# Filters re-read with both planes per transfer, second weights read two rows at a time, first weights taken at column stride two

## The chip, the cores and the metric

The kernel runs on one core of a Trainium2 chip. The core has a matrix engine (TensorE, with its own row for weight loads), VectorE, ScalarE and GpSimd for elementwise work, and SyncE, which issues most of the transfers. The metric is the device time of one execution in microseconds (us); lower is better. In the profile the engines are called PE, PEld (weight loads), DVE, ACT, POOL and SP; a "q" behind an engine's name means its instruction queue rather than its arithmetic, and most transfers have only such a row.

## The reference

Two steps follow one another. The first filters each of 8 sequences of 3008 positions and 256 channels in the frequency domain; the second is a two-layer perceptron with an exact GELU on all 24064 rows.

```python
X = np.fft.rfft(x, axis=1)
F = (filt_r + 1j * filt_i)[None, :, :]
y = np.fft.irfft(X * F, n=x.shape[1], axis=1)     # 8 x 3008 x 256
x = y.reshape(B * S, D)                            # 24064 x 256
h = x @ w_in                                       # 256 x 2048
g = 0.5 * h * (1.0 + erf(h * inv_sqrt2))
return g @ w_out                                   # 2048 x 256
```

## The kernel before

**Filtering.** The transform of length 3008 is split as 47 x 64 and done with matrix products against tables. Sequence 0 goes first, all on its own (functions c1 to c4). Sequences 1 to 7 are worked while TensorE does the perceptron of earlier rows: s1 (product with the 47-point table, L397), a round trip through device memory in the buffer R (written at L407, read back by r1 at L413 into b_sb), s2 (product with the 64-point table T2p, L421, and at L424 the multiplication by the filters F), s3 (L438), a second round trip (written at L450, read back by r2 at L457 into d_sb), and s4 (L466), which writes the filtered rows to a ring buffer, y_sb.

**Filters.** F holds, for each of 24 frequency columns k, two planes t (real and imaginary part) of 256 channels, over 128 partitions. At the start the filters are loaded in one order of partitions, for sequence 0. A copy is saved to device memory (Fd, L106) and later read back in another order by load_filters_again (L113), in groups of 32 partitions. It is called three times during the perceptron of the first rows: for columns 0 to 3, 4 to 7, and 8 to 23.

**Perceptron.** Rows go in 47 tiles of 512. For a tile, mm1 (L580) makes one of 16 blocks of 128 hidden columns per call: two matmuls of 512 columns, one for each half of the 256 input channels, whose weights are 128 columns of w_in_sb; ScalarE applies the GELU into g_sb (L583). The second layer runs one tile behind. For tile 0 it is mm2 (L594), plain. For all others it is mm2_seven (L653): the product is split in 2 x 2 blocks and computed with seven block products instead of eight. The sums over g_sb are made on VectorE (L622, L628, L635), the sums over the weights once, by weight_sums (L608), into w_sums. Each 128-column matmul has its own weight load. The hidden blocks jc = 2i and 2i + 1 form the two halves of the 2 x 2 split.

**Order.** The order is written out by hand. A slot s is one call of mm1; `at[s]` lists what is put ahead of it, then comes the second layer of the tile before (seven 128-column matmuls), then mm1. SP's queue carries the filter reads, b_sb, d_sb, the writes of R and the outputs, in program order. GpSimd's queue carries the loads that convert from float32: x, w_in, w_out. Around slot 12 the order on SP is: 4 writes of R, filters 0 to 3, three b_sb reads, filters 4 to 7, filters 8 to 23.

```python
put(r1 if c < 3 else unit(3) + 1, m.r1, b, c)   # r1 = 12 for b = 1
...
put(11, m.load_filters_again, 0, 4)
put(13, m.load_filters_again, 4, 4)
put(17, m.load_filters_again, 8, 16)
put(17, m.weight_sums)
```

The second weights are loaded by two calls of load_w_out on GpSimd (L138), right after the loads of x for sequence 1. The table T4a is made on GpSimd (L376, L378) in the same stretch, from 49.17 to 73.87 us.

Of the kernel before, what the change touches and what calls it, by code (L numbers as in the profile page):

```python
# [30 lines left out]
class _Mix:  # L31
# [75 lines left out]

    def load_filters_again(self, k0, k):

        for t in range(2):  # L110
            for o in range(0, 128, 32):
                i = self.st["Fd"][o // 64, :, :, t, k0:k0 + k, :].rearrange("q i k c -> (q i) (k c)")
                self.nc.sync.dma_start(out=self.F[o:o + 32, t, k0:k0 + k, :], in_=i)  # L113

    def dup_filters(self, eng, k0, k):
        for k in range(k0, k0 + k, 2):
# [17 lines left out]
            self.nc.gpsimd.dma_start(out=self.w_in_sb[:, dc, :], in_=wi[:, dc, :])  # L134

    def load_w_out(self, j):
        wo = self.w_out.rearrange("(jc p) o -> p jc o", p=128)
        self.nc.gpsimd.dma_start(out=self.w_out_sb[:, j:j + 8, :], in_=wo[:, j:j + 8, :])  # L138


    def iota(self, g, name, shape, pattern, base=0, cm=0, dt=FP32):
# [430 lines left out]
    def mm1(self, t, jc):  # L572
        nc = self.nc
        if jc == 0:
            self.st["g", t] = self.pg.tile([128, 16, TCH], FP16, tag="g", name="g_sb")
        ps = self.bank("ps_h", "h")
        o = 0
        for off, n in self.segs(t):
            for dc in range(2):
                nc.tensor.matmul(ps[:, o:o + n], lhsT=self.w_in_sb[:, dc, jc * 128:jc * 128 + 128],  # L580
                                 rhs=self.ring[:, dc, off:off + n], start=(dc == 0), stop=(dc == 1))
            o += n
        nc.scalar.activation(out=self.st["g", t][:, jc, :], in_=ps, func=AF.Gelu)  # L583
# [330 lines left out]
```

## Time and profile before

| What | Value |
|---|---|
| Median of 4 runs | 753.81 us (752.76 to 754.97) |
| The profiled execution | 752.93 us |
| Its span in the profile | 751.1 us |
| TensorE clock granted | 0.999 of full speed |
| L580, matmuls of the first layer | 417.9 us busy, 1468 recorded |
| L580, weight loads | 1600, 98 ns each |
| L653, matmuls of the second layer | 219 ns each as recorded, groups that overlap |
| Filter reads F<-Fd | 8 of 256 KB (5.8 us to landing), 16 of 64 KB (2.2 us) |
| b_sb<-R | 28 of 384 KB, 4.2 us to landing |
| w_out_sb | 2 of 512 KB, 11.2 us to landing |

The span runs from the first to the last recorded instruction. "Busy" counts the time in which at least one instruction of an engine is running. A matmul's recorded length includes its way through the array, so that matmuls overlap in the record: seven of the second layer, 219 ns each, take 0.55 us together. "To landing" is the median time from a transfer's issue to its arrival. A wait is put down to what came last before the waiting instruction started, by the profile's semaphore events. The whole program of a stage must be read from the timeline of that stage; shares of busy time are averages over all of them.

### The profile page before, as it was taken

To read this page: it belongs to the slowest core of one execution; us is meant where nothing else is said; L and a number is where in the kernel's file an instruction comes from. 1 tells how busy PE (TensorE), PEld (TensorE's weight loads), DVE (VectorE), ACT (ScalarE), POOL (GpSimd) and SP (SyncE) were. 2 spreads that over 40 slices of the span, in tenths; PEclk is the share of its full clock that TensorE was granted. 3 is DMA by queue.
4 is the path that set the end of the run, shared out by engine and by line. 5 is a ranking of instruction groups with operands and counts; after the bars stand their busy time and mean duration, and the time that the engine had idled before them with its cause. 6 is when DMAs were issued, how large, how long until landed. Compare 5 with 4: busy or idle time off the path is not lost.

```text
span 751.1 us, 20124 instructions
## 1 busy us (share of the span) xinstructions
PE 728.3 (97%) x8284; PEld 518.1 (69%) x8420; DVE 593.0 (79%) x1065; ACT 544.6 (73%) x963; POOL 101.9 (14%) x191
## 2 busy tenths in 40 slices
PE   7998999999999999999999999999999999999997
PEld 4845676766776767666677666666677766777776
DVE  7967978897787977789777997779967898675566
ACT  6895678677786777866777667876678767777773
POOL 7969100020001200012000120002100000000000
PEclk9999999999999999999999999999999999999999
DMA  9999663474445652546525457245562433511011
GB/s 146 221 195 271 148 141 93 121 173 103 103 114 154 140 130 84 145 124 127 143 73 161 112 106 169 61 145 123 122 142 76 130 106 86 114 44 42 30 57 58
DMA packets 92605, 90.73 MB, mean 121 GB/s; under 512 B 7904, under 2 KB 79072, under 8 KB 92256
## 3 DMA queue, kind: packets, MB, share of 16 engines
q1 hardware_dynamic: 84128, 73.43, 35.5%
q0 software_dynamic: 8384, 16.00, 14.1%
q8 instruction: 66, 1.08, 0.6%
q14 instruction: 27, 0.22, 0.1%
HBM read 57.15 MB, written 48.23 MB: 140 GB/s over the span
## 4 chain that ended last, share of the span: by engine, by line
PE 86%; DVE 6%; DMA 3%; ACT 2%; issue 2%; SPq 1%; POOL 0%; DVEq 0%; POOLq 0%; ACTq 0%
PE ps_o L653 37%; PE ps_h L580 36%; PE ps_s L466 3%; PE ps_s L438 3%; PE ps_s L421 2%; PE ps_s L397 2%; DVE p L424 2%; DVE s_sb L622 1%; ACT g_sb L583 1%; DMA x_sb<-in_x_dram 1%; DMA F<-Fd 1%; PE ps_c L528 1%; DMA b_sb<-R 1%; DVE ost L682 1%; PE ps_c3t L543 1%
## 5 line engine op out<-in xcount | busy, mean ns | idle before, releaser
L583 ACT ACTIVATE g_sb<-ps_h 128x512 f16<-128x512 f32 x752 | 447.9, 597 | 185.7 <-PE ps_h L580 165.4
L580 PE MATMUL ps_h<-y_sb,w_in_sb 128*128 128x512 bf16 (+3 forms) x1468 | 417.9, 365 | 0.4
L653 PEld LDWEIGHTS <-g_sb 128*128 128x128 f16 x2944 | 193.9, 98 | 80.7 <-issue 15.6
L653 PEld LDWEIGHTS <-s_sb 128*128 128x128 f16 x2208 | 150.2, 98 | 51.3 <-issue 2.9
L580 PEld LDWEIGHTS <-w_in_sb 128*128 128x128 bf16 x1600 | 124.6, 98 | 6.6 <-issue 1.0
L653 PE MATMUL ps_o<-w_sums,g_sb 128*128 128x128 f16 x1472 | 127.1, 219 | 2.0 <-DVE g_sb L628 1.2
L653 PE MATMUL ps_o<-w_sums,s_sb 128*128 128x128 f16 x1472 | 126.5, 219 | 1.3
L622 DVE TENSOR_TENSOR s_sb<-g_sb 128x1024 f16<-128x1024 f16 x184 | 122.9, 691 | 0.0
L653 PE MATMUL ps_o<-w_out_sb,g_sb 128*128 128x128 f16 x1472 | 120.3, 219 | 1.8
L424 DVE TENSOR_TENSOR p<-ps_s,F 128x1024 bf16<-128x1024 f32 x84 | 102.4, 1220 | 24.7 <-PE ps_s L421 14.6
L123 POOL COPY gate<-p 1x1 bf16<-1x1 bf16 x40 | 19.1, 477 | 417.6 <-DVE p L424 417.6
L628 DVE TENSOR_TENSOR g_sb<-s_sb,g_sb 128x1024 f16<-128x1024 f16 x92 | 63.6, 691 | 1.1
L653 PE MATMUL ps_o<-w_out_sb,s_sb 128*128 128x128 f16 x736 | 63.3, 219 | 0.5
L635 DVE TENSOR_TENSOR s_sb<-g_sb 128x1024 f16<-128x1024 f16 x92 | 62.7, 681 | 0.0
L304 DVE TENSOR_SCALAR y_sb<-ps_s 128x376 bf16<-128x376 f32 x56 | 30.5, 545 | 27.9 <-PE ps_s L466 27.9
L675 DVE TENSOR_TENSOR t_sb<-t_sb,ps_o 128x256 f32<-128x256 f32 x46 | 19.2, 417 | 40.0 <-PE ps_o L653 40.0
L466 PEld LDWEIGHTS <-d_sb 96*128 96x128 bf16 x448 | 31.4, 98 | 25.7 <-issue 0.7
L302 DVE CAST a_sb<-ps_s 128x512 bf16<-128x512 f32 x57 | 36.6, 686 | 13.0 <-PE ps_s L397 12.8
L670 DVE TENSOR_TENSOR ost<-t_sb,ps_o 128x256 f32<-128x256 f32 x46 | 19.2, 418 | 31.0 <-PE ps_o L653 31.0
L466 PE MATMUL ps_s<-T4a,d_sb 96*128 96x94 bf16 x448 | 37.2, 206 | 1.8 <-DMA d_sb<-R 0.5
L682 DVE TENSOR_TENSOR ost<-t_sb,ps_o 128x256 f32<-128x256 f32 x90 | 33.6, 414 | 5.6 <-PE ps_o L653 5.6
L421 PE MATMUL ps_s<-b_sb,T2p 128*128 128x256 bf16 x168 | 32.1, 273 | 4.3 <-DMA b_sb<-R 3.2
(147 smaller groups left out, 502.5 us busy)
## 6 DMA issues: line engine op xcount, KB each, us to landing
out_dram<-ost SPq DMA_DIRECT2D x92, 256.0 KB, 2.6
x_sb<-in_x_dram POOLq DMA_DIRECT2D x64, 188.0 KB, 3.8
b_sb<-R SPq DMA_DIRECT2D x28, 384.0 KB, 4.2
R<-v_sb SPq DMA_DIRECT2D x84, 128.0 KB, 2.5
d_sb<-R SPq DMA_DIRECT2D x56, 192.0 KB, 3.9
R<-a_sb SPq DMA_DIRECT2D x108, 96.0 KB, 2.2
F<-Fd SPq DMA_DIRECT2D x8, 256.0 KB, 5.8
Fd<-F SPq DMA_DIRECT2D x8, 192.0 KB, 6.8
```

Source lines behind the costliest of these rows:

```text
L302: self.nc.vector.tensor_copy(out=out, in_=in_)
L304: self.nc.vector.tensor_scalar(out=out, in0=in_, scalar1=scale, scalar2=None, op0=ALU.mult)
L421: nc.tensor.matmul(ps[:, 256 * i:256 * i + 256], lhsT=self.T2p[:, k].rearrange("p a b c d -> p (a b c d)"), rhs=self.st[b, "b", k // 6][:, ...
L424: nc.vector.tensor_tensor(out=w, in0=ps.unsqueeze(1).to_broadcast([128, 2, 512]), in1=self.F[:, :, 2 * p:2 * p + 2, :].rearrange("p t a b ...
L466: nc.tensor.matmul(ps[:, 94 * i:94 * i + 94], lhsT=d[:, (grp % 2) * 4 + i, 128 * half:128 * half + 128], rhs=self.T4a[:, 4 * grp + i], sta ...
L580: nc.tensor.matmul(ps[:, o:o + n], lhsT=self.w_in_sb[:, dc, jc * 128:jc * 128 + 128], rhs=self.ring[:, dc, off:off + n], start=(dc == 0), ...
L583: nc.scalar.activation(out=self.st["g", t][:, jc, :], in_=ps, func=AF.Gelu)
L622: self.nc.vector.tensor_tensor(out=self.st["s", t][:, i:i + 2], in0=a, in1=b, op=ALU.subtract)
L628: self.nc.vector.tensor_tensor(out=a21[:, k], in0=self.st["s", t][:, k, 0], in1=a22[:, k], op=ALU.add)
L635: self.nc.vector.tensor_tensor(out=self.st["s4", t][:, k], in0=a12[:, k], in1=s2[:, k], op=ALU.subtract)
L653: nc.tensor.matmul(ps[:, (m + 1) % 2, sub, :], lhsT=a[:, i, 128 * sub:128 * sub + 128], rhs=b[:, i], start=i == 0, stop=i == 7)
L682: v(out=c(h, 1 - h), in0=tt, in1=p, op=ALU.add)
```

## The change

Three edits. load_filters_again makes one transfer for both planes of 32 partitions instead of one for each plane, so four issues a call instead of eight. load_w_out reads two neighbouring rows of w_out in one run: partition p of block pair i now holds rows 256 i + 2 p and 256 i + 2 p + 1, where before block jc held rows 128 jc + p. So that h has its columns in the same order, mm1 takes every second of 256 weight columns, starting at jc % 2.

```diff
     def load_filters_again(self, k0, k):
-        for t in range(2):
-            for o in range(0, 128, 32):
-                i = self.st["Fd"][o // 64, :, :, t, k0:k0 + k, :].rearrange("q i k c -> (q i) (k c)")
-                self.nc.sync.dma_start(out=self.F[o:o + 32, t, k0:k0 + k, :], in_=i)
+        for o in range(0, 128, 32):
+            i = self.st["Fd"][o // 64, :, :, :, k0:k0 + k, :].rearrange("q i t k c -> (q i) t (k c)")
+            self.nc.sync.dma_start(out=self.F[o:o + 32, :, k0:k0 + k, :], in_=i)
...
     def load_w_out(self, j):
-        wo = self.w_out.rearrange("(jc p) o -> p jc o", p=128)
-        self.nc.gpsimd.dma_start(out=self.w_out_sb[:, j:j + 8, :], in_=wo[:, j:j + 8, :])
+        wo = self.w_out.rearrange("(i p e) o -> p i (e o)", p=128, e=2)
+        self.nc.gpsimd.dma_start(out=self.w_out_sb[:, j:j + 8, :].rearrange("p (i e) o -> p i (e o)", e=2),
+                                 in_=wo[:, j // 2:j // 2 + 4, :])
...
         ps = self.bank("ps_h", "h")
+        w = self.w_in_sb[:, :, 256 * (jc // 2) + jc % 2:256 * (jc // 2) + 256:2]
         o = 0
         for off, n in self.segs(t):
             for dc in range(2):
-                nc.tensor.matmul(ps[:, o:o + n], lhsT=self.w_in_sb[:, dc, jc * 128:jc * 128 + 128],
+                nc.tensor.matmul(ps[:, o:o + n], lhsT=w[:, dc],
                                  rhs=self.ring[:, dc, off:off + n], start=(dc == 0), stop=(dc == 1))
```

## The prediction

> **What bounds the kernel now.** I read the page's first part, then the chain of waits that ended last, then TensorE's waits over the whole run and by stage, and last the timeline of the stage in which the filters come back.
>
> ```profile
> PE 728.3 (97%) x8284; PEld 518.1 (69%) x8420; DVE 593.0 (79%) x1065; ACT 544.6 (73%) x963; POOL 101.9 (14%) x191
> ...
> PE 86%; DVE 6%; DMA 3%; ACT 2%; issue 2%; SPq 1%; POOL 0%; DVEq 0%; POOLq 0%; ACTq 0%
> ```
>
> TensorE is busy 728.3 of 751.1 us, and 86% of the chain is TensorE. So time is lost or won in two ways only: by a wait of TensorE, or by a change in the pace at which it runs. The list of waits has few of the first kind. After 50 us TensorE stands still for long just three times, and the two that matter lie in the stage that the change touches:
>
> ```profile
> PE ps_s L421 <- DMA b_sb<-R: 3.2, 1, 3.2
> PE ps_o L653 <- DVE g_sb L628: 0.8, 1, 0.8
> ```
>
> (Columns: total us, times, longest us; the third is 0.5 us for d_sb, much later.) The first lasts from 55.4 to 58.58 us. What it waits for is seen on SP's own queue, timeline from 44 to 100 us:
>
> ```profile
> 49.34 1.92 SPq L407 DMA_DIRECT2D R<-p  x4
> 51.31 3.71 SPq L113 DMA_DIRECT2D F<-Fd  x8
> 55.12 1.32 SPq L413 DMA_DIRECT2D b_sb<-R  x3
> 56.53 8.36 SPq L113 DMA_DIRECT2D F<-Fd  x16
> ```
>
> SP issues in order. The first eight filter reads take 3.71 us, 0.46 each, and only then comes the b_sb read that TensorE needs. It lands about 3.4 us after its issue (3.3 is the least, 3.6 the median of the first two), at 58.5.
>
> **Part 1, the filters' return.** Each call makes four issues instead of eight: 24 become 12, with the same bytes and the same runs. An issue's cost hardly depends on its bytes (0.42 to 0.46 us apart at 64 KB and at 256 KB), so I price a 128 KB issue at 0.46; a third dimension in the pattern may cost more, and the nearest rows, Fd<-F with its reversed rows, take 0.59 at the median. The first call then takes 4 x 0.46 = 1.84 us, and b_sb can be issued at 51.31 + 1.84 = 53.2 instead of 55.12. Is something else late then? b_sb reads what R<-p wrote. The last of those four is issued at about 50.84 and takes 2.2 us to land: 53.0. So the issue holds at 53.2, 1.9 us earlier. But the 512 KB of the first call now go out in half the time and stand ahead of b_sb in the same queue. Between 64 and 71 us, where nearly only filters move, they run at some 220 GB/s with the engines full. From 51.9 at that rate the 512 KB last until 54.3, so the data of b_sb start about 0.5 us later than on a free queue. Gain at this wait: 1.9 - 0.5 = **1.4 us**. Ends: 0.9 if an issue costs 0.59 (4 x 0.13 = 0.5 less), 1.9 if the backlog does not matter.
>
> The other filters: SP held its sixteenth filter read until 60.87, when the third b_sb landed, and the last call's 2.1 MB landed at 70.7. After the change that call begins some 2 to 3 us earlier and still needs 2.1 MB / 220 GB/s = 9.5 us, so it lands near 68.4. Its first reader is the product of unit 4, which ran on VectorE at 72.96, behind other work of VectorE. Nothing gates there before or after. The chain names 6.25 us of "F<-Fd" ahead of L628, but VectorE had no idle time before L628, and L628 does not read F; I book nothing for it.
>
> What is given back: VectorE runs without a gap from 65.9 to 76 us, and three L622 and one L628 in it take 1.1 to 1.2 us instead of 0.68 while GpSimd makes T4a (49.2 to 73.9). GpSimd's work does not move. With TensorE and VectorE 1.4 us earlier, the next L622 (at 72.32) and L628 (at 74.10), now 0.7 each, come under GpSimd's last operations and may lose 0.45 each. The second L628 is what the 0.8 us wait is for, so 0 to 0.9 goes back into it; I take 0.4. Part 1: -1.4 + 0.4 = **-1.0 us**, between -1.9 and 0.
>
> **Part 2, the second weights in pairs of rows.** Two GpSimd issues (0.90 and 0.92 us) with half the runs. They land 10.0 and 12.4 us after 33.7 and 34.6, the last at 47.0; the first reader, L608, starts at 47.83, just as VectorE is done with the p copies ahead of it. GpSimd then waits 6.4 us for t_sb at 49.17, which hides whatever its issues save or cost. Loads of x are ahead in the queue. Worth 0; without that cover, some tenths of a us. Row order in w_out_sb and column order of h change together, so L608, L653 and the sums keep count and shape.
>
> **Part 3, weight columns at stride two.** No instruction is added. But all 1,600 loads of w_in_sb now step over every second column, and nothing in this trace loads weights with a step. This is the term that decides, because of where the load stands:
>
> ```profile
> 98.31 0.28 PE L653 MATMUL ps_o<-w_out_sb,s_sb 128*128 128x128 f16 x2
> ...
> 98.37 0.15 PEld L580 LDWEIGHTS <-w_in_sb 128*128 128x128 bf16 x2
> 98.42 0.38 PE L580 MATMUL ps_h<-y_sb,w_in_sb 128*128 128x512 bf16 x1
> ```
>
> (Timeline; columns: start us, us, what. Groups of x2 start some 0.055 us apart.) A load starts when the matmul before it starts. The second load of a slot has a 512-column matmul over it (0.215 us from start to start): twice its 98 ns would still be hidden. The first has only the last 128-column matmul of L653, 0.055 us. There are 720 such slots (tiles 2 to 46, sixteen each), so every 10 ns not hidden cost 7.2 us. Bounds by rows of the same engine:
>
> ```profile
> L580 PEld LDWEIGHTS <-w_in_sb 128*128 128x128 bf16 x1600 | 124.6, 98 | 6.6 <-issue 1.0 <-DMA x_sb<-in_x_dram 0.4
> ...
> L438 PEld LDWEIGHTS <-U 64*64 64x64 bf16 x336 | 7.9, 106 | 13.1 <-issue 8.9
> ...
> L356 PEld LDWEIGHTS <-T2g 128*96 128x96 bf16 x1 | 0.1, 119 | 0.0
> ```
>
> (After the bar: busy us, mean ns of one.) The 128-column load is faster than the 96-column one: full-width loads go a quicker way. Without it, 64 and 96 columns give 13 ns per 32, so 128 would take 132, 34 more than now. Exposed in full that is 720 x 34 = 24.5 us; exposed not at all, 0. A gain has a reason against it: same number of weights, and the array's 55 ns per matmul is the pace.
>
> [...]
>
> **Sum and rivals.** Against the profiled execution (752.93 us, its span 751.1 and 1.8 around it): -1.0 + 0 + 0 = 751.9. The median of the four runs, 753.81, is 0.9 above that execution, so the forecast is **752.8**.
>
> - A, the forecast, 0.56: stepped loads stay hidden; 751.2 to 754.3.
> - B, slower, 0.27: stepped loads leave the quick way, 132 ns, and the first load of each slot shows: 752.8 + 24.5 = 777. For: the one stage that repeats 720 times has 55 ns of cover, and the quick way has conditions. Against: a record may outlast the matmul's start. It decides from some 5 ns exposed per slot (3.3 us).
> - C, slower still, 0.12: weights arrive at half pace, 52 ns exposed: 752.8 + 37 = 790.
> - D, faster, 0.05: both waits vanish, 3.2 + 0.8: 749.8. Against: the issue can come only 1.9 us sooner.
>
> That the change does nothing at its place would be 753.8: the weight load of L421 is put down to GpSimd's T4a, not to a DMA, yet L421 does not read T4a and the landing of b_sb fits to 0.1 us. It lies inside A.
>
> A measurement of this kernel tells about 0.3% (2.3 us) from no change. Faster by more: D and 0.09 of A. Within: 0.45 of A. Slower: B, C and 0.02 of A. The range runs from 750.5 to 779, leaving out C and D.
>
> **What would show it.** Right: wait of L421 near 1.8 us, b_sb issued near 53.2, the wait for L628 0.8 to 1.7, w_in_sb loads still near 98 ns and slots still 0.82 us. Wrong: loads of 110 ns or more with L580's first matmul later than 0.055 us after L653's last (B, C), or b_sb issued early yet landing near 58.5.

## The result and the profile after

The changed kernel takes 752.57 us (median of 36 runs, 750.63 to 755.03) against 754.29 us for the kernel before (57 runs, 751.90 to 755.65): a ratio of 0.9981, 95% interval 0.9975 to 0.9987. By the ratio it is 1.4 us faster (the medians differ by 1.7); that is less than a single measurement of this kernel could tell, and is seen only because many runs were made. The two profiled executions do not show it: 752.93 us (span 751.1) before, 753.03 us (span 751.2) after. The profile of before was one of its quick executions, 1.4 us under its median, and that of after lies 0.5 us above its own. So the profiles have to be read stage by stage, and the gain must be looked for in more than these two.

The page of the changed kernel, busy times and then the chain of waits that ended last, by engine:

```profile
PE 728.4 (97%) x8284; PEld 518.0 (69%) x8420; DVE 593.3 (79%) x1065; ACT 544.7 (73%) x963; POOL 101.7 (14%) x191
...
PE 86%; DVE 5%; DMA 5%; ACT 2%; issue 1%; POOL 0%; SPq 0%; DVEq 0%; POOLq 0%; ACTq 0%
```

TensorE does the same work in the same time. Only the small shares of the chain moved: transfers went from 3% to 5%, SP's queue from 1% to 0%. The waits of TensorE in the stage of the filters (total us, times, longest us):

```profile
PE ps_s L422 <- DMA b_sb<-R: 2.7, 1, 2.7
PE ps_o L655 <- DVE g_sb L630: 2.1, 2, 1.7
```

The first was 3.2 us and the second 0.8: 0.5 us won, 1.3 us of other waiting added (0.9 in the longest one). SP's queue in the same stage, timeline from 44 to 82 us:

```profile
49.39 1.93 SPq L408 DMA_DIRECT2D R<-p  x4
51.36 2.48 SPq L112 DMA_DIRECT2D F<-Fd  x4
54.02 1.40 SPq L414 DMA_DIRECT2D b_sb<-R  x3
55.46 6.37 SPq L112 DMA_DIRECT2D F<-Fd  x8
```

Four filter reads now take 2.48 us, 0.62 each, where eight took 3.71, 0.46 each. So b_sb is issued at 54.02 instead of 55.12, 1.1 us sooner, and the issue of all later filters ends at 61.8 instead of 64.9. The wait after this is seen on VectorE, timeline from 44 to 82 us (in brackets: the idle time just before, and what ended it):

```profile
63.64 1.23 DVE L425 TENSOR_TENSOR p<-ps_s,F 128x1024 bf16<-128x1024 f32 x1 [1.97 <-DMA F<-Fd]
...
73.55 1.22 DVE L425 TENSOR_TENSOR p<-ps_s,F 128x1024 bf16<-128x1024 f32 x1 [0.54 <-DMA F<-Fd]
74.69 0.68 DVE L630 TENSOR_TENSOR g_sb<-s_sb,g_sb 128x1024 f16<-128x1024 f16 x1
```

Before, the same two lines read:

```profile
72.96 1.23 DVE L424 TENSOR_TENSOR p<-ps_s,F 128x1024 bf16<-128x1024 f32 x1
74.10 0.68 DVE L628 TENSOR_TENSOR g_sb<-s_sb,g_sb 128x1024 f16<-128x1024 f16 x1
```

The product of the filters for unit 4, at 73.55, waits for the last filters and pushes the second L630 behind it to 74.69; TensorE waits 1.75 us for that. The chain through this stretch (start us, length, what) names the same two transfers:

```profile
54.99 6.27 DMA b_sb<-R
61.26 0.02 issue
61.28 12.15 DMA F<-Fd
...
73.55 1.22 DVE p L425
74.77 0.61 DVE g_sb L630
75.38 0.05 issue
75.43 0.51 PE ps_o L655 x6
```

The third b_sb read, issued at 54.99, lands at 61.26, and only then, at 61.28, does SP issue the last of the twelve filter reads; that read lands at 73.4, and the rest hangs on it. Before, the last of the 24 reads was issued at 64.5 and landed at 72.7, and the same product ran at 72.96. The filters therefore come back no sooner, although they are asked for some 3 us sooner. From the first filter read to unit 4's product it was 72.96 - 51.31 = 21.65 us before and is 73.55 - 51.36 = 22.19 after: by these two profiles alone the change would be a loss of half a microsecond. The next s3 begins 8.1 us behind that product in both (81.08 and 81.67), and from it to the end of the span both take 669.5 to 670 us, so in these two profiles this product decides; in some of those below it takes up to 1.7 us more to come from it to the next s3. Times in this stage are counted from the first filter read, because that read itself begins anywhere from 49.7 to 51.5 us in the profiles that share its place.

### The profile page after: what moved, and what is told of

It is laid out like the page before. It is cut to its first block, busy times and chain, and to the rows that moved or that the text cites. A ratio compares the mean times of both kernels' runs of the same rounds, so it can differ in the third digit from the quotient of the medians.

```text
span 751.2 us, 20104 instructions
## 1 busy us (share of the span) xinstructions
PE 728.4 (97%) x8284; PEld 518.0 (69%) x8420; DVE 593.3 (79%) x1065; ACT 544.7 (73%) x963; POOL 101.7 (14%) x191
## 4 chain that ended last, share of the span: by engine, by line
PE 86%; DVE 5%; DMA 5%; ACT 2%; issue 1%; POOL 0%; SPq 0%; DVEq 0%; POOLq 0%; ACTq 0%
PE ps_o L655 37%; PE ps_h L582 36%; PE ps_s L467 3%; PE ps_s L439 3%; PE ps_s L422 2%; PE ps_s L398 2%; DVE p L425 2%; DMA F<-Fd 2%; ACT g_sb L585 1%; DVE s_sb L624 1%; DMA b_sb<-R 1%; DMA x_sb<-in_x_dram 1%; PE ps_c L529 1%; DMA F<-in_filt_i_dram 1%; DVE ost L684 1%
## 5 line engine op out<-in xcount | busy, mean ns | idle before, releaser
L655 PEld LDWEIGHTS <-g_sb 128*128 128x128 f16 x2944 | 193.9, 98 | 81.6 <-issue 15.6
L582 PEld LDWEIGHTS <-w_in_sb 128*128 128x128 bf16 x1600 | 124.6, 98 | 6.6 <-issue 1.0
L425 DVE TENSOR_TENSOR p<-ps_s,F 128x1024 bf16<-128x1024 f32 x84 | 102.4, 1220 | 24.8 <-PE ps_s L422 21.3
L630 DVE TENSOR_TENSOR g_sb<-s_sb,g_sb 128x1024 f16<-128x1024 f16 x92 | 63.6, 691 | 1.1
```

What stands on the lines that cost most here:

```text
L425: nc.vector.tensor_tensor(out=w, in0=ps.unsqueeze(1).to_broadcast([128, 2, 512]), in1=self.F[:, :, 2 * p:2 * p + 2, :].rearrange("p t a b ...
L582: nc.tensor.matmul(ps[:, o:o + n], lhsT=w[:, dc], rhs=self.ring[:, dc, off:off + n], start=(dc == 0), stop=(dc == 1))
L630: self.nc.vector.tensor_tensor(out=a21[:, k], in0=self.st["s", t][:, k, 0], in1=a22[:, k], op=ALU.add)
L655: nc.tensor.matmul(ps[:, (m + 1) % 2, sub, :], lhsT=a[:, i, 128 * sub:128 * sub + 128], rhs=b[:, i], start=i == 0, stop=i == 7)
```

## Experiments: which part carries the gain

**One part at a time.** Three kernels, each the kernel before with part of the change. The filters' return alone (f_only):

```diff
-        for t in range(2):
-            for o in range(0, 128, 32):
-                i = self.st["Fd"][o // 64, :, :, t, k0:k0 + k, :].rearrange("q i k c -> (q i) (k c)")
-                self.nc.sync.dma_start(out=self.F[o:o + 32, t, k0:k0 + k, :], in_=i)
+        for o in range(0, 128, 32):
+            i = self.st["Fd"][o // 64, :, :, :, k0:k0 + k, :].rearrange("q i t k c -> (q i) t (k c)")
+            self.nc.sync.dma_start(out=self.F[o:o + 32, :, k0:k0 + k, :], in_=i)
```

> Only the filters' return is changed (12 issues of both planes); the second weights and the weight columns stay as before. Theory T (the gain comes from b_sb being issued sooner): the ratio to before is that of the whole change, about 0.998, and the wait of TensorE for b_sb is near 2.7 us instead of 3.2. Rival R (the filters' return gives back at the product of unit 4 what it wins at b_sb, and the gain comes from the weights): 1.000 within 0.0007, with the wait for b_sb 0.5 us shorter and the wait for L628 about 0.9 us longer.

Measured: 752.40 us beside 753.96, ratio 0.9979 (0.9970 to 0.9987).

The weights alone (pairs of rows and the stepped columns, the filters' return as before; w_only):

```diff
+        wo = self.w_out.rearrange("(i p e) o -> p i (e o)", p=128, e=2)
...
+        w = self.w_in_sb[:, :, 256 * (jc // 2) + jc % 2:256 * (jc // 2) + 256:2]
```

> Only the weights are changed: pairs of rows of w_out and columns of w_in at stride two; the filters come back in 24 issues as before. Theory T: 1.000 within 0.0007, weight loads of 98 ns. Rival R: about 0.998, with something shorter before 55 us. A third, B (stepped loads cost something hidden in the sum of the change): 1.001 or more, and slots of the steady part longer than 0.82 us.

Measured: 754.46 us beside 753.96, ratio 1.0003 (0.9993 to 1.0012).

The stepped columns alone, with the second weights in their old order, so that h and the second weights do not match (stride_only):

```diff
+        w = self.w_in_sb[:, :, 256 * (jc // 2) + jc % 2:256 * (jc // 2) + 256:2]
...
+                nc.tensor.matmul(ps[:, o:o + n], lhsT=w[:, dc],
```

> Weight columns of w_in at stride two, with w_out read row by row as before: the hidden columns then meet other rows of w_out, so this leaves out the matching order and is read for its time alone. Theory that stepped loads are free (the prediction): 1.000 within 0.0007, 98 ns per load, the first matmul of L580 0.055 us after the last of L653. Theory B: loads of up to 132 ns, 1.003 to 1.03.

Measured: 754.24 us beside 753.96, ratio 0.9995 (0.9985 to 1.0004). The page's row of the weight loads in this kernel (busy us, mean ns of one, then the idle time before them):

```profile
L581 PEld LDWEIGHTS <-w_in_sb 128*128 128x128 bf16 x1600 | 124.6, 98 | 6.6 <-issue 1.5
```

98 ns, busy 124.6 us, the same as with packed columns. So the stepped loads cost nothing that shows, the second weights bring nothing that shows (both within 0.15%), and the whole gain belongs to the filters' return.

## Experiments: where in the filters' return

**The reads moved ahead** (early). If what matters is that the filters stand ahead of b_sb on SP, the first two calls can go earlier, while SP has less to do:

```diff
-    put(11, m.load_filters_again, 0, 4)
-    put(13, m.load_filters_again, 4, 4)
+    put(4, m.load_filters_again, 0, 4)
+    put(7, m.load_filters_again, 4, 4)
```

> The change, with the filters of columns 0 to 3 called at slot 4 and those of columns 4 to 7 at slot 7, ahead of the writes of R that follow there, instead of slots 11 and 13; columns 8 to 23 stay at slot 17. If b_sb is late only because filter reads stand ahead of it in SP's queue and on the transfer engines: b_sb is issued when the last write of R has landed (near 53.2 us), lands 3.3 us later, TensorE goes on near 56.6 instead of 58.1, and the last filters land near 67 to 68, so that the product of unit 4 does not wait: 1.5 to 2.8 us less than before, ratio 0.9965 to 0.998. If the transfer engines are the limit from 40 us on, the writes of R land later, s1 is delayed and the ratio stays at 0.998 or goes above.

Measured: 755.84 us beside 753.96, ratio 1.0023 (1.0013 to 1.0034): slower. SP's queue of this kernel, timeline from 36 to 66 us:

```profile
45.89 3.16 SPq L112 DMA_DIRECT2D F<-Fd  x4
49.15 2.04 SPq L408 DMA_DIRECT2D R<-a_sb  x4
51.28 2.46 SPq L112 DMA_DIRECT2D F<-Fd  x4
53.85 2.03 SPq L408 DMA_DIRECT2D R<-p  x4
57.75 1.29 SPq L414 DMA_DIRECT2D b_sb<-R  x3
```

SP has too little idle time ahead of slot 12: in after the twelve writes R<-a_sb took 7.48 us, of which some 2 us were waiting, and the eight filter reads need 5. They now stand ahead of R<-p, where after has none of them; R<-p starts at 53.85 instead of 49.39, and b_sb, which reads what those wrote, at 57.75. TensorE's wait for it grew to 6.2 us.

**The same two calls before the hand-written order begins** (start2):

```diff
+    m.load_filters_again(0, 4)
+    m.load_filters_again(4, 4)
     at = {}
```

> The change, with the filter reads of columns 0 to 7 moved in program order ahead of the loop of slots, so that SP issues them before the first write of R, where its queue is empty. If SP's issue time is what made the run with slots 4 and 7 slower: b_sb is issued near 53.2, lands near 56.6, and the ratio is 0.9960 to 0.9975. If these 1 MB delay x or w_out, which load at the same time: s1 starts later than 39.5 or the sums over the weights start later than 48, and the ratio is 0.998 or more.

Measured: 754.54 us beside 753.96, ratio 1.0005 (0.9996 to 1.0014). The twelve writes R<-a_sb took 10.64 us instead of 7.48 and R<-p again came late (52.09), so b_sb was issued at 55.95 and TensorE waited 4.2 us. The second case of the expectation came true in part: s1 was not late (38.98), but the second weights were. Their last transfer landed at 51.39 instead of 47.02, and their sums began at 51.48 instead of 47.79, after VectorE had waited 4.07 us for them; SP meanwhile waited 7.9 us for earlier transfers to land before it could issue all writes of R. So the reads, issued even earlier, took their time from the transfers beside them.

**b_sb ahead of all filters** (b_first):

```diff
-    put(11, m.load_filters_again, 0, 4)
+    put(12, m.load_filters_again, 0, 4)
```

> The change, with the filter reads of columns 0 to 3 put behind the three b_sb reads (slot 12) instead of ahead of them. b_sb is issued near 53.2 and lands near 56.6, but then the filters of unit 0 land near 59 to 60 and VectorE waits for them. If TensorE's wait sets the end, 0.997; if the product of units 0 to 4 does, since it waits for filters in any order, 0.998 to 1.000.

Measured: 754.66 us beside 753.96, ratio 1.0011 (0.9999 to 1.0023). VectorE's timeline in this kernel:

```profile
62.06 1.23 DVE L425 TENSOR_TENSOR p<-ps_s,F 128x1024 bf16<-128x1024 f32 x1 [10.89 <-DMA F<-Fd]
...
74.68 1.22 DVE L425 TENSOR_TENSOR p<-ps_s,F 128x1024 bf16<-128x1024 f32 x1 [0.71 <-DMA F<-Fd]
```

b_sb now went out at 53.34 and TensorE waited only 1.7 us for it, the shortest so far. But the product of unit 0 had to wait for the filters until 62.06, the later products came after it, and L630 made TensorE wait 2.5 us. A shorter first wait alone wins nothing.

**Half of the last filters on ScalarE's queue** (act_half; filters_part is the loop of load_filters_again with the queue and the groups of partitions as arguments):

```diff
-    put(17, m.load_filters_again, 8, 16)
+    put(17, m.filters_part, nc.sync, 8, 16, (0, 32))
+    put(26, m.filters_part, nc.scalar, 8, 16, (64, 96))
```

> The change, with the last call of the filters' return (columns 8 to 23) split over two queues: partitions 0 to 63 stay on SP at slot 17, partitions 64 to 127 are issued by ScalarE at slot 26. Theory P (after the change the product of unit 4 sets the pace, it waits for the last filters, and these move at 220 GB/s because each transfer goes to 32 partitions): the two halves move side by side, the last filters land near 68 instead of 73.4, the wait for them is gone and 0.5 to 1.5 us with it: ratio 0.9962 to 0.9975. Rival: the transfer engines as a whole are the limit, or ScalarE loses as much by issuing: 0.998 or more.

Measured: 753.70 us beside 753.74, ratio 1.0009 (0.9994 to 1.0024). Unit 4's product still waited 0.62 us for the filters. The transfer engines were full (DMA share 1.02 to 1.15 in each window of 2 us from 56 to 66 us), and the second queue moved the data no faster: 222 and 209 GB/s in the windows from 60 to 64 us, where after moved 209 to 220 from 62 to 70. So there was no gain to set against the 1.0 us by which the two issues (1.27 us on ScalarE's queue) held up a GELU.

**The last filters left out** (no_f3). This kernel is after without the third call: it leaves out 2.1 MB of reads, columns 8 to 23 keep the first order of partitions, and it is read for its time alone:

```diff
-    put(17, m.load_filters_again, 8, 16)
```

> The change, without the read-back of columns 8 to 23, so that the products of units 4 to 11 use the filters in the old order of partitions: it leaves out 2.1 MB and four issues, and is read for its time alone. Theory P: the upper bound of what earlier filters can bring; the product of unit 4 does not wait, and the ratio is 0.9955 to 0.997. Rival (VectorE's own queue or TensorE's pace sets the time of unit 4): 0.9975 to 0.9985.

Measured: 751.97 us beside 753.74, ratio 0.9978 (0.9968 to 0.9988). The landing is gone, yet this is hardly quicker than after (0.9981). Taken alone, it says that the last filters do not matter. The profiles that follow show why that is too short.

## Experiments: the clock, and two limits in series

**The kernel before, profiled a second time** (before_copy, no edit):

> The kernel before, for a second profile of it. The first profile showed no fall of the clock, while most timed executions have a mean clock of 0.995 to 0.997 and are 1 to 2 us longer. If the wait for b_sb is what makes the clock fall in those: this profile, with a mean clock of 0.997 or less (three in four), shows half the clock for 3 to 7 us after 56 us, and the product of unit 4 near 74.4 instead of 73.0. If the lower means come from elsewhere (the start or the end): full clock between 50 and 70 us at the same mean.

Measured: 753.87 us in one run, span 752.1. TensorE's timeline from 54 to 66 us:

```profile
54.77 0.60 PE L594 MATMUL ps_o<-w_out_sb,g_sb 128*128 128x256 f16 x4
...
58.46 0.59 PE L421 MATMUL ps_s<-b_sb,T2p 128*128 128x256 bf16 x2 [2.65 <-DMA b_sb<-R]
58.84 1.06 PE L594 MATMUL ps_o<-w_out_sb,g_sb 128*128 128x256 f16 x4
59.69 1.06 PE L580 MATMUL ps_h<-y_sb,w_in_sb 128*128 128x512 bf16 x2
```

Four matmuls of L594 take 0.60 us ahead of the wait and 1.06 us behind it. The windows of the same stretch, whose third column from the right is the granted clock:

```profile
58.00:60.00 2.00, 1.54 (x7) 1.02 (x8) 0.92 (x1) 0.00 (x0) 1.92 (x3) 0.54 1.06 400
60.00:62.00 2.00, 2.00 (x9) 1.05 (x8) 0.67 (x2) 0.60 (x1) 1.84 (x3) 0.60 0.73 181
62.00:64.00 2.00, 2.00 (x17) 1.41 (x16) 1.56 (x2) 1.19 (x2) 1.92 (x3) 1.00 1.02 268
```

The profile of before that the prediction was made from shows 1.00 in all of these windows, and so does after's. In this second profile of the same kernel TensorE ran at half clock for 3.4 us between 58 and 62 us (the shortfalls of 0.46 and 0.40 in two windows of 2 us, at a clock of 0.50), and unit 4's product came at 74.15, 22.89 us after the first filter read instead of 21.65. So 1.2 us of this execution came from a fall of the clock that the first profile did not have. It is the usual case as far as the mean granted clock tells. Of the 14 profiles made here, the six with a mean of 0.999 or more show no fall in this stage, the five with 0.997 or 0.998 show one of 3.4 us, and the three with 0.995 show one of 6.8 us. Executions of the two kernels by this mean, and the mean of their times:

| Mean granted clock | before | after |
|---|---|---|
| 0.999 or more | 12 of 106, 752.60 us | 12 of 37, 752.17 us |
| 0.996 to 0.998 | 66 of 106, 753.93 us | 22 of 37, 752.59 us |
| 0.995 or less | 28 of 106, 754.67 us | 3 of 37, 754.63 us |

**Keeping TensorE busy through the wait.** Eight matmuls on a table of ones, into a bank that nobody reads, were put ahead of s2, once in before (before_warm) and once in after (after_warm):

```diff
+    def keep_warm(self, n):
+        ps = self.bank("ps_keep")
+        for i in range(n):
+            self.nc.tensor.matmul(ps, lhsT=self.ones[:, 0:128], rhs=self.ones, start=True, stop=True)
...
+    put(22, m.keep_warm, 8)
```

> The kernel before, with eight idle 512-column matmuls on ones (1.7 us) put into TensorE's wait for b_sb at slot 22; they write a bank that nothing reads. Theory G (in many executions the wait of 3.2 us and more makes the granted clock fall to half for some 7 us, and the change wins by making that rarer): the clock does not fall, the wait ends at the same time, and most of the gain of the change comes without it: ratio 0.998 to 0.9985, mean clocks of 0.998 to 1.0 where before has mostly 0.997 and 0.995. Rival T (the gain is the shorter wait itself): 1.000 within 0.0007.

> The change, with the same eight matmuls in the wait for b_sb, which is 2.7 us there. Theory G: the remaining executions with a lower clock (12 of 37 at 0.997 or less) are gone, so 0.997 to 0.998 to before, some 0.3 to 0.8 us under the change. Rival T: no difference from the change, 0.998.

Measured: in before 754.30 us beside 753.96, ratio 0.9999 (0.9989 to 1.0008), in after 753.04, ratio 0.9984 (0.9973 to 0.9995): no gain over the kernel without them in either. In before the eight did not keep the clock up: its profile shows 0.79, 0.50 and 0.85 in the three windows from 58 to 64 us. In after they did behind the wait for b_sb, with 1.00 in all windows up to 74 us; but there, behind its second wait, the clock fell:

```profile
74.00:76.00 2.00, 2.00 (x13) 1.20 (x11) 2.00 (x3) 0.60 (x1) 2.00 (x6) 0.50 0.79 147
76.00:78.00 2.00, 2.00 (x15) 1.37 (x14) 1.46 (x3) 0.60 (x1) 0.52 (x2) 0.64 1.12 178
```

The waits of TensorE there:

```profile
PE ps_o L660 <- DVE g_sb L635: 2.5, 2, 2.2
...
PE ps_s L427 <- DMA b_sb<-R: 0.5, 1, 0.5
```

The wait for b_sb is down from 2.7 to 0.5 us, most of it because the eight matmuls themselves take 1.9, and the other one has grown to 2.2: unit 4's product stood 1.10 us for the filters. Here, then, the last filters are the limit, where in the kernel without the third call their absence brought little, because that one's profile shows half clock from 56 to 62 us (0.79, 0.50, 0.85).

**Both taken away** (no_f3_warm). Two limits that stand one behind the other would explain why neither edit alone brought anything. The kernel that tests it is after with the eight matmuls and without the third call of load_filters_again:

```diff
+    put(22, m.keep_warm, 8)
...
-    put(17, m.load_filters_again, 8, 16)
```

> After, without the third call of load_filters_again (columns 8 to 23 are not read back, so 16 of 24 filter columns stay in the first order) and with the eight idle matmuls ahead of s2. Theory S (two limits in series, each hiding behind the other: with the clock fall and the wait for b_sb gone the landing of the last filters gates unit 4's product, with the filters gone the wait and the clock do): neither edit alone won over after (0.9984 and 0.9978 beside 0.9981), both together do: no half clock between 56 and 66 us, unit 4's product 20.3 to 21.3 us after the first filter issue (after: 22.2, after_warm 21.8, no_f3 22.0), median 750.7 to 751.7, ratio to before 0.9955 to 0.9970. Rival T (unit 4's product is held by the order and pace of TensorE and VectorE anyway, so that neither limit is worth anything beyond after): ratio 0.9975 to 0.9987, product at 21.5 us or later although no F wait is left.

Measured: 751.64 us beside 754.05, ratio 0.9968 (0.9958 to 0.9978). The waits of TensorE, and then two windows of it:

```profile
PE ps_o L660 <- DVE g_sb L635: 1.6, 2, 1.3
PE ps_s L427 <- DMA b_sb<-R: 0.7, 1, 0.7
```

```profile
58.00:60.00 2.00, 2.00 (x16) 1.41 (x15) 1.64 (x2) 1.19 (x2) 1.84 (x3) 1.00 0.90 222
60.00:62.00 2.00, 2.00 (x16) 1.41 (x15) 0.77 (x1) 1.19 (x2) 1.86 (x3) 1.00 0.15 48
```

No half clock, no wait for filters, and the product of unit 4 came 20.65 us after the first filter read (70.34 - 49.69), inside the expected 20.3 to 21.3. All nine executions had a mean clock of 0.999 or more. The median is 1.4 us below after_warm, but only 0.33 us below no_f3, and the interval of the ratio reaches into the rival's, so the profiles are needed beside it. For all kernels that share the order of the stage, the way from the first filter read to unit 4's product splits in two at the moment when TensorE goes on behind the wait for b_sb; the last column goes on to the next s3 (us):

| Kernel | First filter read to TensorE going on | Half clock after it | Product waits for filters | From there to the product | From the product to the next s3 |
|---|---|---|---|---|---|
| before, first profile | 7.27 | no | no | 14.38 | 8.12 |
| stepped columns alone | 7.38 | no | no | 14.32 | 8.12 |
| before, second profile | 7.20 | yes | no | 15.69 | 8.11 |
| weights alone | 7.26 | yes | no | 15.71 | 8.11 |
| before, eight matmuls | 7.22 | yes | no | 15.63 | 8.11 |
| filters' return alone | 6.35 | no | 0.46 | 14.28 | 8.91 |
| after, both taken away | 6.35 | no | no | 14.30 | 8.66 |
| after | 6.71 | no | 0.54 | 15.48 | 8.12 |
| after, eight matmuls | 6.09 | behind the product | 1.10 | 15.70 | 9.78 |
| after, no last filters | 6.48 | yes | no | 15.53 | 8.10 |
| after, half on ScalarE | 6.10 | yes | 0.62 | 16.61 | 8.12 |

The first stretch takes 7.20 to 7.38 us with the old return (mean of five 7.27) and 6.09 to 6.71 with the new one (mean of six 6.35): **0.9 us won**, without overlap between the two groups. The second takes 14.3 us if nothing stands in the way, 15.5 to 15.7 with a half clock or with late filters, and 16.6 with both. The filters' return alone waits 0.46 us for filters and still needs only 14.28: in that execution they landed early enough. So up to the product each limit is worth some 1.2 to 1.4 us, and a kernel that sheds one can still meet the other.

The last column shows that a part is given back behind the product. It is 8.1 us but for three profiles. With the eight matmuls in after it comes with the fall of the clock shown above. In the other two the product came early, and the sum over g_sb behind it fell under GpSimd's last work on T4a; in the filters' return alone:

```profile
72.47 0.97 POOL L377 TENSOR_TENSOR T4a<-t_sb 96x376 bf16<-96x376 f32 x1
...
72.52 1.47 DVE L627 TENSOR_TENSOR g_sb<-s_sb,g_sb 128x1024 f16<-128x1024 f16 x1
```

It took 1.47 us, and 1.23 with both limits taken away, where it takes 0.68 in before and in after. Over the whole way from the first filter read to the next s3, the profiles with the old return take 29.8 us at full clock and 31.0 with a fall; the filters' return alone takes 29.5, both taken away 29.3, and after 30.3. At full clock there is thus little to win here, and the times by mean clock say the same: 0.4 us (752.60 to 752.17), which a dozen executions on each side do not clear of their spread.

No tried version that computes the whole result is quicker than the changed kernel or its filters' part alone.

## Why the prediction was right, and where its steps were not

The forecast, 752.8 us and 1.0 us below the median of before, is met: 752.57, and 1.4 us below by the ratio. The steps behind it fared unequally.

- **Part 3, the stepped weight loads: 0, confirmed.** The one term that could have cost 24 or 37 us costs nothing: 98 ns a load, ratio 0.9995. Rivals B and C fall. No run shows the 52 ns that C exposes in each slot, nor the 37 us it makes of them: with the step the loads are as long as before.
- **Part 2, the second weights in pairs: 0, confirmed** as far as it can be told: with the step, 1.0003 (0.9993 to 1.0012). The packets of the software queue did fall by 1024, to 7360.
- **Part 1, the place: right.** The gain is all in the filters' return, as is shown by f_only. D, both waits gone, fell: no kernel lost both.
- **Part 1, the gain at the wait: 0.9 us, its lower end.** Two terms were mis-sized. "I price a 128 KB issue at 0.46"; it took 0.62 (0.59 for the record itself), so b_sb went out 1.13 us sooner relative to the first filter read (2.67 instead of 3.80), not 1.9. The alternative in the text, 0.59 from the reads with reversed rows, was the right row. The backlog ahead of b_sb in the engines was put at 0.5 us; it came to 0.2 (7.27 - 3.80 = 3.47 from issue to TensorE before, 6.35 - 2.67 = 3.68 after). 1.13 - 0.2 = 0.9. The forecast for the wait itself, 1.8, was missed with them: 2.7 in after's profile.
- **Part 1, "Nothing gates there before or after": wrong.** The text let the last filters land at 70.7 before, and near 68.4 after. They landed at 72.7 and 73.4. The first was misread: 70.7 is not the last landing, and unit 4's product at 72.96 was already within 0.3 us of it. The second took the sooner start of the call for a sooner end: the last issue waited for the third b_sb read until 61.28, and its 512 KB then stood behind the other three. The chain's 6.25 us of filters ahead of L628, which the prediction set aside, pointed at this limit. after_warm and no_f3_warm bound what it is worth: without the third call the median is 1.4 us lower (753.04 to 751.64), which includes the fall of the clock behind the wait that the late filters caused.
- **The give-back: right in kind and size; its cause differs from profile to profile.** It was taken as 0.4 (0 to 0.9), from GpSimd slowing two VectorE operations. So it was where the product came early: 0.8 us in f_only and 0.5 in no_f3_warm, from the sum that took 1.47 and 1.23 us instead of 0.68 (the table's last column). In after's own profile that sum took 0.68; the longest wait for L630 grew by 0.9 there, and what came last before it was the filters' landing.
- **Not in the prediction at all: the clock.** Its profile had a granted clock of 0.999 and the stage at full pace. A half-clock stretch behind the wait for b_sb, 1.3 us long in its effect, is in three of the five profiles with the old return, and one is in three of the six with the new one.

So -1.0 was met by other sums than those written, and in part by luck: 0.9 won at the wait, as the lower end had it, and then a second stretch that takes 14.3 or 15.6 us by chance of clock and landing, of which the prediction knew nothing. What is **shown** is that the filters' return alone carries the gain, that TensorE goes on 0.9 us sooner behind the first filter read in every profile with the new return, and that the clock's fall and the filters' landing can each cost 1.2 to 1.4 us between there and the product. **Open** is how this comes to 1.4 us at the end, since behind the product some of it is given back. The table by mean clock allows an estimate: if before had after's shares of the three groups, its mean would be 753.56 us instead of 753.97. By that, 0.4 us comes from rarer falls, the long ones above all (28 of 106 against 3 of 37), and 0.9 us at like clock. It is not a test: before_warm, which was to tell the clock apart, kept its half clock in the profile. One fall costs 1.3 us in before (752.60 to 753.93) and only 0.4 in after (752.17 to 752.59); this fits a fall that hides behind the late filters, though in act_half's profile the two added up to 16.6 us. Whether reading back first those columns that unit 4 needs would lift the second limit was not tried.

## What to carry to other kernels

Here fewer issues helped only the transfer that waits behind them on the same queue (b_sb, issued 1.1 us sooner), and the pattern with a further dimension took part of it back (0.62 us an issue instead of 0.46); count the issues ahead of the late one at the price of their own form. When the last piece of a transfer group is held back or the transfer engines are full, as here, asking for it earlier does not bring it earlier: the last filters were asked for some 3 us sooner and landed at 73.4 us instead of 72.7. Follow a gain to the end of its stage: of what f_only had won at the product, 0.8 us was gone at the next s3. And when an edit that removes an evident limit brings nothing, look for the second limit behind it and remove both at once, in a kernel that leaves the work out, before the first is called harmless.

## What the runs showed of the hardware

- **The clock fell at a wait of 2.2 us and held at one of 3.4, and a fall lasted 3.4 or 6.8 us.** Half clock (0.50 in the lowest windows) came with waits of TensorE of 2.2 (after_warm, the second wait), 2.3 (before_warm), 2.4 (act_half), 2.65 (before_copy), 2.9 (no_f3), 4.2 (start2), 4.4 (w_only) and 6.2 us (early); none came with waits of 3.4 (stride_only), 3.2 (before), 2.7 (after and f_only) and 2.5 us (b_first, the second wait). Added up from the shortfalls in windows of 2 us, it lasted 3.4 us in the first five and 6.8 us in the other three. So between 2.2 and 3.4 us the length of the wait alone does not tell whether the clock falls, and the runs here do not say what else does.
- **An issue on SP took 0.46 us for a two-dimensional filter read and 0.62 us for a three-dimensional one**, from one issue to the next in the first call of before and of after (3.71 us for eight, 2.48 for four). The size hardly shows in the records themselves: 0.42 us at the median for 256 KB and for 64 KB in before, 0.59 for 128 KB and 0.57 for 512 KB in after.
- **Reads into 32 partitions moved about 210 GB/s with the transfer engines full**: the four 512 KB reads of after landed 2.3 to 2.6 us apart (66.0, 68.3, 70.9, 73.4), at a DMA share of 0.94 to 1.06 in the windows of 2 us from 64 to 72 us.
- **Weight loads of 128 bf16 columns at a step of two took 98 ns in after and in stride_only**, as the packed ones did in before.
